# The second product of a fused FFN kernel turned round: weights stationary, activations moving, in 64x64 tiles

## The chip, the cores and the metric

The kernel runs on one core of a Trainium2 chip. The metric is the device time of one execution in microseconds. The kernel before takes 2056.47 us, the median of three runs (2056.41 to 2056.66).

## What is computed

Two layers in a row, all inputs and outputs in float32. The first is a short dynamic convolution: for each of 32768 tokens and each of 8 heads a softmax over 7 taps weighs the last 7 rows of x. The second is a feed-forward layer with a squared ReLU:

```python
w = softmax(weight_gen)                      # (8, 4096, 8, 7)
out = einsum('bshk,bskhg->bshg', w, x_unf)   # (8, 4096, 192): 7 taps, 24 channels to a head
h = out.reshape(32768, 192) @ w_in           # first product, (32768, 2048)
g = maximum(h, 0) ** 2
y = g @ w_out                                # second product, (32768, 192)
```

The accuracy of float32 is kept by splitting each factor into a high and a low float16 part. Each product is then the sum of three float16 products (high by high, low by high, high by low).

## The kernel before

**Tiling.** Token row `p * 256 + r` lies on partition `p`, so a partition holds 256 consecutive tokens. A chunk is `TC` = 4 values of `r`, or 512 tokens, and there are `NCH` = 64 chunks. Each chunk `c` has four blocks `b` = 0 to 3, and each block has two units `j`; a unit covers 256 of the 2048 hidden columns.

**The work of one unit.**
- `mm1(c, j)` (L412) makes the first product on TensorE. The 192 channels are folded to 64 partitions times 3, so each matmul has 64 rows, and the two halves `i` of the array (rows 0 to 63 and 64 to 127) make two blocks of hidden columns at once. The weights `W` are stationary (64x128), the transposed activations `xh`, `xl` move, 512 tokens wide.
- ScalarE does `relu` (L431), `square` (L435) and `high` (L439, the high float16 part `gh`). VectorE does `low` (L443, the low part `gl`).
- `mm2(c, b)` (L458) makes the second product for both units of a block. Here the activations `gh`, `gl` are stationary (64x128, 128 tokens wide) and the weights `V` move, 192 output channels wide. The result lies with tokens on the partitions. The two halves `h` of the hidden block go to the two row halves of the array and to two PSUM banks of the accumulator `acc[t // 2]`.

**The end of a chunk.** `finish(c, p)` (L482) runs once for each of the two accumulators. ScalarE copies one bank out, scaled by `f` (L493, into `tmp`); VectorE adds the other bank, scaled by `f`, and writes `o_sb` (L494). `f` is a scale for each partition, made by `descale` (L147). `store` (L496) issues one DMA for the chunk.

**The convolution of a later chunk** runs on VectorE in between: softmax steps (L289 to L293), seven multiplications and six additions of 128x768 (L306, L312), then from chunk 4 on a transpose in 32x32 blocks (L394), a round trip through DRAM to complete the transpose (`xd`, L400, and `xT`, L405), and the split into `xh` on ScalarE (L346) and `xl` on VectorE (L352). Chunks 0 to 3 are transposed on TensorE instead (L375), in float32, with weights of 128x64: two column halves of the array at once.

**The order of the work** is written out by hand in the last loop (L660 to L713). Every engine runs its instructions in that order. In iteration (c, b): the two `mm1` of the block; on VectorE the two `low` left over from the block before (`late`); if b = 1, the two `finish` and the `store` of chunk c - 1; then `mm2` of the block before; then the ScalarE steps; then the pieces of the convolution that a table (`todo`) has for this place. So `mm2(c, 0)` stands behind `finish(c - 1)` and needs its accumulators, which have one buffer each. All DMAs are issued on SyncE's queue (SP), in order.

Of the kernel before, what the change touches and what calls it, by code (L numbers as in the profile page):

```python
# [8 lines left out]
F32 = mybir.dt.float32  # L9
# [20 lines left out]
def kernel(  # L30
# [9 lines left out]
    nc = tc.nc  # L40
# [87 lines left out]
    def size_steps(gi):  # L128
# [15 lines left out]

        return total, scales

    def descale(gi):  # L147
        f = falls[gi] = att.tile([P, 1], F32, name="f", bufs=3)
        d = downs.pop(gi)
        stt(out=f, in0=d, scalar=back, in1=d, op0=ALU.mult, op1=ALU.mult)  # L150

    raws = {}

# [254 lines left out]


    phs, rgs, ghs, gls, accs = {}, {}, {}, {}, {}  # L410

    def mm1(c, j):  # L412
        ph = phs[c, j] = ps_h.tile([P, 2, N], F32, name="ph")
        if c == 0:
            w = wfull[j // 2].rearrange("p j n -> p (j n)").rearrange("p (k j n) -> p k j n", k=ND, j=2)
            seq = [(w, xts[0]["x"], k) for k in range(ND)]
        else:
            xh, xl = xts[c]["h"], xts[c]["l"]
            seq = [(W[:, q, j // 2], xx, k) for q, xx in ((0, xh), (0, xl), (1, xh)) for k in range(ND)]
        for n, (w, xx, k) in enumerate(seq):  # L420
            for i in range(2):
                rows = slice(i * D1, (i + 1) * D1)
                fl = dict(start=(n == 0), stop=(n == len(seq) - 1))
                nc.tensor.matmul(ph[:, i], w[rows, k, j % 2], xx[rows, k], **fl)  # L424

    def relu(c, j):
        r = rgs[c, j] = gp.tile([P, 2, N], F32, name="g", bufs=NJ)
# [27 lines left out]
            o = accs[0][t // 2][:, t % 2, 0:D]  # L455
            nc.tensor.matmul(o, rgs[0, j][:, i, t * P:(t + 1) * P], v, start=fb == 0, stop=fb == NF - 1)  # L456

    def mm2(c, b, ts_=range(TC)):  # L458
        if b == 0 and 0 in ts_:
            new_accs(c)  # L460
        j0, j1 = 2 * b, 2 * b + 1
        order = [(t, j) for t in ts_ for j in (j0, j1)]
        if c == NCH - 1 and b == NB - 1:
            order = [(t, j) for j in (j0, j1) for t in range(TC)]
        for t, j in order:
            for i in range(2):
                fb = block(j, i)
                first, last = fb == 0 and t % 2 == 0, fb == NF - 1 and t % 2 == 1
                for n, g in enumerate((ghs[c, j], ghs[c, j], gls[c, j])):
                    for h in range(2):  # L470
                        rows = slice(h * D1, (h + 1) * D1)
                        nc.tensor.matmul(  # L472
                            accs[c][t // 2][:, h, t % 2 * D:(t % 2 + 1) * D],
                            g[rows, i, t * P:(t + 1) * P], V[rows, fb, n * D:(n + 1) * D],
                            start=first and n == 0, stop=last and n == 2,
                        )
        for j in (j0, j1) if TC - 1 in ts_ else ():
            del ghs[c, j], gls[c, j]

    outs = {}  # L480

    def finish(c, p):  # L482
        if p == 0:
            outs[c] = op.tile([P, TC, D], F32, name="o_sb")
        o = outs[c][:, 2 * p:2 * p + 2]
        acc = accs[c][p]
# [5 lines left out]
        tmp = op.tile([P, 2 * D], F32, name="tmp")  # L492
        act(tmp, acc[:, 1, 0:2 * D], AF.Copy, scale=f)  # L493
        stt(out=o, in0=acc[:, 0, 0:2 * D], scalar=f, in1=tmp, op0=ALU.mult, op1=ALU.add)  # L494

    def store(c, p0=0, p1=2):  # L496
        nc.sync.dma_start(
# [162 lines left out]
    for c in range(1, NCH + 1):  # L660
        for b in range(NB if c < NCH else 2):
# [20 lines left out]
            if b == 1:  # L682
                for p in range(2):
                    finish(c - 1, p)
                    if c == NCH:
                        store(c - 1, p, p + 1)
                if c < NCH:
                    store(c - 1)
            turn = turns.pop(c + 1, None) if b == NB - 1 else None
            if b == NB - 1 and c + 1 in splits and turn is None:  # L690
# [3 lines left out]
                mm2(*pend.pop(0))  # L694
            elif pend:
                one = pend.pop(0)
                mm2(*one, range(TC // 2))
                turn()
                mm2(*one, range(TC // 2, TC))
            if c < NCH:  # L700
                relu(c, js[0])
                square(c, js[0])
# [41 lines left out]
```

## Time and profile before

The profiled execution took 2056.41 us, 2054.6 us of it from the first to the last instruction (the span).

| engine | busy us | share of the span |
|---|---|---|
| TensorE, matmul (PE) | 2044.6 | 100% |
| TensorE, weight load (PEld) | 1492.7 | 73% |
| VectorE (DVE) | 1762.3 | 86% |
| ScalarE (ACT) | 1755.1 | 85% |
| the 16 DMA engines, hardware queue | | 25.2% |

Busy times of matmuls overlap, since several run in the array at once and each is recorded to the end of its pipeline. How fast they follow each other is read from when groups start. Rows named PEld are weight loads. In a row such as `64*128 64x192 f16`, the first pair is the part of the array (rows by columns), the second is what moves through it (partitions by columns). SPq is SyncE's queue; its rows are the issue of DMAs, not the transfers.

### The profile page before, as it was taken

To read this page: it belongs to the slowest core of one execution; us is meant where nothing else is said; L and a number is where in the kernel's file an instruction comes from. 1 tells how busy PE (TensorE), PEld (TensorE's weight loads), DVE (VectorE), ACT (ScalarE), POOL (GpSimd) and SP (SyncE) were. 2 spreads that over 40 slices of the span, in tenths; PEclk is the share of its full clock that TensorE was granted. 3 is DMA by queue.
4 is the path that set the end of the run, shared out by engine and by line. 5 is a ranking of instruction groups with operands and counts; after the bars stand their busy time and mean duration, and the time that the engine had idled before them with its cause. 6 is when DMAs were issued, how large, how long until landed. Compare 5 with 4: busy or idle time off the path is not lost.

```text
span 2054.6 us, 73890 instructions
## 1 busy us (share of the span) xinstructions
PE 2044.6 (100%) x33814; PEld 1492.7 (73%) x33814; DVE 1762.3 (86%) x2310; ACT 1755.1 (85%) x2010; POOL 10.5 (1%) x14
## 2 busy tenths in 40 slices
PE   9999999999999999999999999999999999999999
PEld 6777777777777777777777777777777777777777
DVE  8999888888888888888888888888888888888873
ACT  6788888888888888888888888888888888888887
POOL 2000000000000000000000000000000000000000
PEclk9999999999999999999999999999999999999999
DMA  6112221332312322213323123222133231232220
GB/s 186 41 63 81 87 65 62 95 95 64 95 41 86 95 72 87 77 51 94 95 64 95 45 82 95 72 87 83 45 95 92 67 95 48 80 95 72 56 63 18
DMA packets 98073, 158.34 MB, mean 77 GB/s; under 512 B 8168, under 2 KB 60776, under 8 KB 93792
## 3 DMA queue, kind: packets, MB, share of 16 engines
q1 hardware_dynamic: 97760, 153.61, 25.2%
q8 instruction: 264, 4.33, 0.9%
q14 instruction: 49, 0.40, 0.1%
HBM read 104.82 MB, written 48.76 MB: 75 GB/s over the span
## 4 chain that ended last, share of the span: by engine, by line
PE 98%; DVE 2%; SPq 0%; DMA 0%; issue 0%; ACT 0%; POOL 0%; DVEq 0%; POOLq 0%
PE acc L472 49%; PE ph L424 48%; PE acc L456 1%; DVE pr L306 0%; DVE pr L312 0%; PE ph L375 0%; DVE W L262 0%; SPq L117 0%; DMA xt<-in_x_dram 0%; DVE gl L443 0%; DVE xl L352 0%; DVE du L199 0%; ACT xh L346 0%; DVE V L262 0%; DVE o_sb L494 0%
## 5 line engine op out<-in xcount | busy, mean ns | idle before, releaser
L472 PE MATMUL acc<-V,gh 64*128 64x192 f16 x16128 | 1018.5, 243 | 0.0
L472 PE MATMUL acc<-V,gl 64*128 64x192 f16 x8064 | 991.7, 243 | 0.2 <-DVE gl L443 0.2
L443 DVE SCALAR_TENSOR_TENSOR gl<-gh,g 128x1024 f16<-128x1024 f16 x504 | 613.2, 1223 | 232.8 <-ACT gh L439 232.6
L424 PEld LDWEIGHTS <-W 64*128 64x128 f16 x9072 | 437.6, 94 | 478.8 <-DVE xl L352 0.8
L424 PE MATMUL ph<-xh,W 64*128 64x512 f16 x6048 | 776.3, 376 | 0.5 <-DVE xl L352 0.5
L472 PEld LDWEIGHTS <-gh 64*128 64x128 f16 x16128 | 728.7, 94 | 59.8 <-issue 0.3
L431 ACT ACTIVATE g<-ph 128x1024 f32<-128x1024 f32 x504 | 511.0, 1014 | 252.7 <-PE ph L424 252.6
L435 ACT ACTIVATE g<-g 128x1024 f32<-128x1024 f32 x512 | 538.8, 1052 | 8.1
L439 ACT ACTIVATE gh<-g 128x1024 f16<-128x1024 f32 x504 | 530.1, 1052 | 8.0
L306 DVE TENSOR_TENSOR pr<-xt,wt 128x768 f32<-128x768 f32 x449 | 421.4, 951 | 2.9 <-DMA xt<-in_x_dram 0.8
L424 PE MATMUL ph<-xl,W 64*128 64x512 f16 x3024 | 408.7, 376 | 0.0
L472 PEld LDWEIGHTS <-gl 64*128 64x128 f16 x8064 | 392.5, 94 | 0.5 <-DVE gl L443 0.5
L312 DVE TENSOR_TENSOR pr<-pr 128x768 f32<-128x768 f32 x384 | 364.5, 949 | 2.3
L352 DVE TENSOR_TENSOR xl<-xT,xh 128x512 f16<-128x512 f32 x180 | 113.5, 685 | 21.0 <-ACT xh L346 21.0
L346 ACT CAST xh<-xT 128x512 f16<-128x512 f32 x180 | 98.4, 609 | 0.0
L494 DVE SCALAR_TENSOR_TENSOR o_sb<-acc,f,tmp 128x384 f32<-128x384 f32 x126 | 71.6, 609 | 3.3 <-ACT tmp L493 3.3
L493 ACT ACTIVATE tmp<-acc,f 128x384 f32<-128x384 f32 x126 | 65.2, 566 | 3.3 <-PE acc L472 3.3
L394 DVE STREAM_TRANSPOSE xr<-pr 128x768 f32<-128x768 f32 x60 | 58.7, 978 | 2.1
L137 ACT ACTIVATE junk<-xt 128x1536 bf16<-128x1536 f32 (+1 forms) x32 | 47.3, 1478 | 0.0
L286 DVE SCALAR_TENSOR_TENSOR wt<-wt,up,sm 128x224 f32<-128x224 f32 x63 | 28.5, 452 | 2.2
L291 ACT ACTIVATE wt<-wt 128x224 f32<-128x224 f32 x64 | 24.0, 375 | 7.3 <-DVE wt L290 7.2
L290 DVE TENSOR_TENSOR wt<-wt,mx 128x224 f32<-128x224 f32 x64 | 25.1, 392 | 2.2
(66 smaller groups left out, 326.0 us busy)
## 6 DMA issues: line engine op xcount, KB each, us to landing
xT<-xd SPq DMA_DIRECT2D x120, 384.0 KB, 5.0
xt<-in_x_dram SPq DMA_DIRECT2D x31, 1344.0 KB, 9.2
out_dram<-o_sb SPq DMA_DIRECT2D x63, 384.0 KB, 5.5
xd<-xr SPq DMA_DIRECT2D x240, 96.0 KB, 2.1
wt<-in_weight_gen_dram SPq DMA_DIRECT2D x31, 224.0 KB, 5.8
raw<-in_moe_w_in_dram SPq DMA_DIRECT2D x8, 384.0 KB, 9.6
raw<-in_moe_w_out_dram SPq DMA_DIRECT2D x4, 768.0 KB, 4.4
xt<-in_x_dram SPq DMA_DIRECT2D x2, 384.0 KB, 5.2
```

The costliest lines, as they stand in the source:

```text
L306: tt(out=dst, in0=src, in1=wk.broadcast_to([P, (t1 - t0) * H, G]), op=ALU.mult)
L312: tt(out=prs[k0][:, part], in0=prs[k0][:, part], in1=prs[k][:, part], op=ALU.add)
L346: nc.scalar.copy(xh, xs)
L352: tt(out=xl, in0=xs, in1=xh, op=ALU.subtract)
L424: nc.tensor.matmul(ph[:, i], w[rows, k, j % 2], xx[rows, k], **fl)
L431: act(r, phs.pop((c, j)), AF.Relu, scale=RHO * LIFT ** 0.5)
L435: act(r, r, AF.Square)
L439: act(gh, rgs[c, j], AF.Copy, scale=1.0 / LIFT)
L443: stt(out=gl, in0=ghs[c, j], scalar=-LIFT, in1=rgs.pop((c, j)), op0=ALU.mult, op1=ALU.add)
L472: nc.tensor.matmul(accs[c][t // 2][:, h, t % 2 * D:(t % 2 + 1) * D], g[rows, i, t * P:(t + 1) * P], V[rows, fb, n * D:(n + 1) * D], start= ...
L493: act(tmp, acc[:, 1, 0:2 * D], AF.Copy, scale=f)
L494: stt(out=o, in0=acc[:, 0, 0:2 * D], scalar=f, in1=tmp, op0=ALU.mult, op1=ALU.add)
```

## The change

It concerns chunks 4 to 62 (`turned`). In these, `mm2_turned` makes the second product with `V` as the stationary operand in pieces of 64x64, and `gh`, `gl` moving. The output channels now lie on the partitions. 128 of the 192 channels go through four matmuls with 512 tokens each (two row halves by two column halves of the array, into `accs[c][0]`); the last 64 channels go through four matmuls with 256 tokens each, one column half for each half of the tokens (into `accs[c][1]`). `mm1` of these chunks is cut into 64x64 pieces too, so all matmuls use one tiling.

`finish` no longer scales. ScalarE copies one bank to `tmp`, VectorE adds the other and writes `s`, 512 columns for the first accumulator and 256 for the second. `store_turned` then turns `s` in 32x32 blocks on VectorE, multiplies by the scale, and stores in 24 DMAs whose contiguous pieces are 32 floats. The scale is needed in another layout (`fs`), which `descale` makes by one DMA to DRAM and four back, for each group of two chunks. `mm2` can now be split by unit where it was split by token tile.

```diff
     def descale(gi):
...
+        if gi * CPG >= N_PE:
+            fd = dram.tile([P], F32, name="fd")
+            fs = spread_falls[gi] = att.tile([P, 1, P // Q, 1], F32, name="fs", bufs=3)
+            nc.sync.dma_start(out=fd.rearrange("(p a) -> p a", a=1), in_=f)
+            for m in range(P // Q):
+                nc.sync.dma_start(
+                    out=fs[m * Q:(m + 1) * Q, 0, :, 0], in_=fd.rearrange("(q i) -> i q", i=Q)
+                )
...
+    HALVES = slice(0, D1), slice(D1, P)
+    def turned(c):
+        return N_PE <= c < NCH - 1
     def mm1(c, j):
...
+        cols = HALVES if turned(c) else (slice(0, P),)
         for n, (w, xx, k) in enumerate(seq):
-            for i in range(2):
-                rows = slice(i * D1, (i + 1) * D1)
-                fl = dict(start=(n == 0), stop=(n == len(seq) - 1))
-                nc.tensor.matmul(ph[:, i], w[rows, k, j % 2], xx[rows, k], **fl)
+            fl = dict(start=(n == 0), stop=(n == len(seq) - 1))
+            for col in cols:
+                for i in range(2):
+                    rows = HALVES[i]
+                    nc.tensor.matmul(ph[col, i], w[rows, k, j % 2, col], xx[rows, k], **fl)
...
+    def mm2_turned(c, j):
+        if j == 0:
+            new_accs(c)
+        gh, gl = ghs.pop((c, j)), gls.pop((c, j))
+        for i in range(2):
+            fb = block(j, i)
+            for n, g in enumerate((gh, gh, gl)):
+                fl = dict(start=fb == 0 and n == 0, stop=fb == NF - 1 and n == 2)
+                for col in HALVES:
+                    for r, rows in enumerate(HALVES):
+                        d = n * D + col.start
+                        nc.tensor.matmul(accs[c][0][col, r], V[rows, fb, d:d + D1], g[rows, i], **fl)
+                for m, col in enumerate(HALVES):
+                    for r, rows in enumerate(HALVES):
+                        d = n * D + P
+                        nc.tensor.matmul(
+                            accs[c][1][col, r, 0:N // 2], V[rows, fb, d:d + D1],
+                            g[rows, i, m * N // 2:(m + 1) * N // 2], **fl,
+                        )
...
     def finish(c, p):
+        acc = accs[c][p]
+        if turned(c):
+            if p == 0:
+                sums_t[c] = op.tile([P, TC * D], F32, name="s", bufs=1)
+            n0, n1 = ((0, N), (N, N + N // 2))[p]
+            n = n1 - n0
+            tmp = op.tile([P, N], F32, name="tmp")
+            nc.scalar.copy(tmp[:, 0:n], acc[:, 1, 0:n])
+            tt(out=sums_t[c][:, n0:n1], in0=acc[:, 0, 0:n], in1=tmp[:, 0:n], op=ALU.add)
+            return
...
+    def store_turned(c):
+        o = op.tile([P, TC * D], F32, name="o_sb")
+        nc.vector.transpose(o, sums_t.pop(c))
+        ob = o.rearrange("p (a q j) -> p a q j", q=P // Q, j=Q)
+        tt(out=ob, in0=ob, in1=spread_falls[c // CPG].broadcast_to(ob.shape), op=ALU.mult)
+        for col in range(0, D, Q):
+            for t in range(TC):
+                if col < P:
+                    p0, n0 = col, t * P
+                else:
+                    p0, n0 = 2 * t // TC * D1 + col - P, N + t % 2 * P
+                nc.sync.dma_start(
+                    out=out_v[:, c * TC + t, col:col + Q].rearrange("(q i) j -> i q j", i=Q),
+                    in_=o[p0:p0 + Q, n0:n0 + P].rearrange("i (q j) -> i q j", j=Q),
+                )
```

Three places show how the instructions move. The first is TensorE where a first product ends and the second product of the block before begins, in the middle of the kernel. Before (L424 is `mm1`, L472 is `mm2`):

```order
L424 MATMUL ph<-xh,W 128x512
L472 LDWEIGHTS gh
L472 MATMUL acc_17189<-V,gh 128x192
L472 LDWEIGHTS gh
L472 MATMUL acc_17189<-V,gh 128x192
L472 LDWEIGHTS gh
L472 MATMUL acc_17189<-V,gh 128x192
L472 LDWEIGHTS gh
L472 MATMUL acc_17189<-V,gh 128x192
L472 LDWEIGHTS gl
L472 MATMUL acc_17189<-V,gl 128x192
```

and now (L440 is `mm1`, L485 and L489 are `mm2_turned`; the lines of the changed file are further down):

```order
L440 MATMUL ph<-xh,W 64x512
L485 LDWEIGHTS V
L485 MATMUL acc_18595<-gh,V 64x512
L485 LDWEIGHTS V
L485 MATMUL acc_18595<-gh,V 64x512
L485 LDWEIGHTS V
L485 MATMUL acc_18595<-gh,V 64x512
L485 LDWEIGHTS V
L485 MATMUL acc_18595<-gh,V 64x512
L489 LDWEIGHTS V
L489 MATMUL acc_18596<-gh,V 64x256
```

What was eight matmuls of 192 columns for one 128-column block of hidden units and one of the three terms is now four of 512 and four of 256; both accumulators are written from the start of the block.

The second place is VectorE at the end of a chunk, in block b = 1 of the next one. Before:

```order
L443 SCALAR_TENSOR_TENSOR gl<-gh,g 128x1024 x2
L494 SCALAR_TENSOR_TENSOR o_sb<-acc_20468,f,tmp 128x384
L494 SCALAR_TENSOR_TENSOR o_sb<-acc_20469,f,tmp 128x384
L292 TENSOR_REDUCE sm<-wt 128x32
L293 TENSOR_SCALAR sm<-sm 128x32
L293 RECIPROCAL sm<-sm 128x32
```

and now:

```order
L459 SCALAR_TENSOR_TENSOR gl<-gh,g 128x1024 x2
L532 TENSOR_TENSOR s<-acc_24412,tmp 128x512
L532 TENSOR_TENSOR s<-acc_24413,tmp 128x256
L548 STREAM_TRANSPOSE o_sb<-s 128x768
L550 TENSOR_TENSOR o_sb<-o_sb,fs 128x768
L302 TENSOR_REDUCE sm<-wt 128x32
L303 TENSOR_SCALAR sm<-sm 128x32
L303 RECIPROCAL sm<-sm 128x32
```

Two instructions became four, in the same place; what follows them is as before.

The third is SyncE's queue over two chunks. Before:

```order
L400 DMA xd<-xr 32x6x128 x4
L405 DMA xT<-xd 64x3x512 x2
L497 DMA out_dram<-o_sb 128x768
L109 DMA wt<-in_weight_gen_dram 128x448
L110 DMA xt<-in_x_dram 128x2688
```

and now:

```order
L415 DMA xT<-xd 64x3x512 x2
L557 DMA out_dram<-o_sb 32x4x32 x24
L156 DMA fd<-f 128x1
L158 DMA fs<-fd 32x4x1 x4
L410 DMA xd<-xr 32x6x128 x4
L415 DMA xT<-xd 64x3x512 x2
L557 DMA out_dram<-o_sb 32x4x32 x24
L109 DMA wt<-in_weight_gen_dram 128x448
L110 DMA xt<-in_x_dram 128x2688
```

One store became 24, and in every second chunk the five small transfers of the scale stand between a chunk's stores and the next chunk's `xd`.

More of the change, by code (lines that the diff above doesn't have):

```diff
@@ L145, in size_steps @@
         return total, scales
+    spread_falls = {}
     def descale(gi):
@@ L456, in mm2_first, with mm2 @@
             nc.tensor.matmul(o, rgs[0, j][:, i, t * P:(t + 1) * P], v, start=fb == 0, stop=fb == NF - 1)
-    def mm2(c, b, ts_=range(TC)):
+    def mm2_turned(c, j):
[17 more added lines that the diff above has]
+                        )
+    def mm2(c, b, half=None):
+        j0, j1 = 2 * b, 2 * b + 1
+        if turned(c):
+            for j in (j0, j1) if half is None else (j0 + half,):
+                mm2_turned(c, j)
+            return
+        ts_ = range(TC) if half is None else range(half * TC // 2, (half + 1) * TC // 2)
         if b == 0 and 0 in ts_:
             new_accs(c)
-        j0, j1 = 2 * b, 2 * b + 1
         order = [(t, j) for t in ts_ for j in (j0, j1)]
@@ L478, in mm2 @@
             del ghs[c, j], gls[c, j]
-    outs = {}
+    outs, sums_t = {}, {}
     def finish(c, p):
+        acc = accs[c][p]
+        if turned(c):
+            if p == 0:
[5 more added lines that the diff above has]
+            tt(out=sums_t[c][:, n0:n1], in0=acc[:, 0, 0:n], in1=tmp[:, 0:n], op=ALU.add)
+            return
         if p == 0:
@@ L485, in finish @@
         o = outs[c][:, 2 * p:2 * p + 2]
-        acc = accs[c][p]
         if c == 0:
@@ L491, in finish @@
         o = o.rearrange("p t d -> p (t d)")
-        tmp = op.tile([P, 2 * D], F32, name="tmp")
-        act(tmp, acc[:, 1, 0:2 * D], AF.Copy, scale=f)
-        stt(out=o, in0=acc[:, 0, 0:2 * D], scalar=f, in1=tmp, op0=ALU.mult, op1=ALU.add)
+        tmp = op.tile([P, N], F32, name="tmp")
+        act(tmp[:, 0:2 * D], acc[:, 1, 0:2 * D], AF.Copy, scale=f)
+        stt(out=o, in0=acc[:, 0, 0:2 * D], scalar=f, in1=tmp[:, 0:2 * D], op0=ALU.mult, op1=ALU.add)
+    def store_turned(c):
[13 more added lines that the diff above has]
+                )
     def store(c, p0=0, p1=2):
@@ L686 @@
                         store(c - 1, p, p + 1)
-                if c < NCH:
+                if turned(c - 1):
+                    store_turned(c - 1)
+                elif c < NCH:
                     store(c - 1)
@@ L696 @@
                 one = pend.pop(0)
-                mm2(*one, range(TC // 2))
+                mm2(*one, 0)
                 turn()
-                mm2(*one, range(TC // 2, TC))
+                mm2(*one, 1)
             if c < NCH:
```

## The prediction, made before the changed kernel was run

> **What bounds the kernel now.** I read the page's busy line first, then the chain that ended last, then that chain as a list in time, and only then single rows.
>
> ```profile
> PE 2044.6 (100%) x33814; PEld 1492.7 (73%) x33814; DVE 1762.3 (86%) x2310; ACT 1755.1 (85%) x2010; POOL 10.5 (1%) x14
> PE 98%; DVE 2%; SPq 0%; DMA 0%; issue 0%; ACT 0%; POOL 0%; DVEq 0%; POOLq 0%
> ```
>
> The chain is TensorE from end to end. As a list (start, length, what), from the middle of the kernel:
>
> ```profile
> 1007.14 3.96 PE acc L472 x96
> 1011.11 3.88 PE ph L424 x36
> 1014.99 3.96 PE acc L472 x96
> ...
> 1054.21 3.96 PE acc L472 x96
> ```
>
> A block is 36 matmuls of the first product (3.88 us) and 96 of the second (3.96 us), with nothing in between: 7.845 us, four to a chunk. Other engines matter only where they would make TensorE wait. Whether it streams at full rate is read from the steps. Two matmuls run side by side, one in each row half. So the first product makes 18 steps of 512 columns in 3.88 us, 215.6 ns each; the second makes 48 steps of 192 columns in 3.965 us (1007.14 to 1011.11 and 1014.99 to 1018.95), 82.6 ns each. Between them lie 320 columns and 133 ns: 0.416 ns a column, and 2.8 ns that every step costs whatever its width.
>
> **TensorE after the change.** The columns stay the same. For one block of hidden units and one term, before: 4 steps of 192 = 768 columns; after, if four 64x64 matmuls run side by side: one step of 512 and one of 256 = 768. Only the number of steps falls, from 48 to 24 in a block's second product. A step of 256 takes 256 x 0.416 + 2.8 = 109.2 ns, so the second product takes 12 x (215.6 + 109.2) = 3.90 us in place of 3.965: 0.067 us less. The first product has twice the matmuls, four in a step instead of two, and the same 18 steps: no change. 59 chunks (4 to 62) have 236 blocks: 236 x 0.067 = 15.8 us. That is all there is to gain.
>
> It needs two things that this kernel does not do now: four matmuls at once, and weight loads of 64 columns hidden beneath them. The nearest rows are TensorE's transposes of the early chunks, with two column halves at once, and the loads of today:
>
> ```profile
> 10.01 0.14 PEld L375 LDWEIGHTS acc<-ident,pr 128*64 128x64 f32 x2 [0.97 <-DVE pr L312]
> 10.01 0.33 PE L375 MATMUL acc<-ident,pr 128*64 128x128 f32 x2 [0.78 <-DVE pr L312]
> ...
> 58.29 2.84 PE L375 MATMUL ph<-ident,pr 128*64 128x128 f32 x48 [0.67 <-DVE pr L312]
> ...
> 1008.05 0.10 PEld L472 LDWEIGHTS <-gl 64*128 64x128 f16 x2
> ...
> L472 PEld LDWEIGHTS <-gh 64*128 64x128 f16 x16128 | 728.7, 94 | 59.8 <-issue 0.3
> L375 PEld LDWEIGHTS acc<-ident,pr 128*64 128x64 f32 x144 | 7.8, 137 | 2.0 <-DVE pr L312 1.9
> L375 PE MATMUL ph<-ident,pr 128*64 128x128 f32 x144 | 8.5, 274 | 0.7 <-DVE pr L312 0.7
> L456 PEld LDWEIGHTS acc<-du,g 128*128 128x128 f32 x128 | 20.7, 190 | 1.4 <-DVE du L198 0.8 <-issue 0.6
> ```
>
> Two loads into different column halves, each of 137 ns or so, lie within 0.14 us: they start some 7 ns apart and run together. Two loads into different row halves, 94 ns each, lie within 0.10 us. The 48 float32 matmuls last 2.84 us: with the length of the last one, 0.27 us, taken off, 24 pairs at 107 ns, which is 128 columns at twice 0.416 ns. So two column halves stream at full rate, with a load of 64 columns for each pair member in every 107 ns, though one load takes 137: loads run ahead. A step of 256 lasts 109 ns and asks for the same in each column half, with the two row halves beside it, as today. How many ns a load holds up the next one is therefore 2 to 7 by these rows; four of them, 28 ns, fit under 109. The other end: 64 columns more make a load 53 ns longer (137 to 190). If loads stood in line with 53 ns each, four would take 212 ns, which fits under a step of 512 and not under one of 256. I take the near end, full rate.
>
> [...]
>
> **VectorE and ScalarE.** The rows for the finish, first the durations and then VectorE's tightest place, just ahead of the 1054.21 above:
>
> ```profile
> L494 DVE SCALAR_TENSOR_TENSOR o_sb<-acc,f,tmp 128x384 f32<-128x384 f32 x126 | 71.6, 609 | 3.3 <-ACT tmp L493 3.3
> L352 DVE TENSOR_TENSOR xl<-ph,xh 128x512 f16<-128x512 f32 x9 | 5.7, 684 | 7.8 <-ACT xh L346 7.8
> L306 DVE TENSOR_TENSOR pr<-xt,wt 128x768 f32<-128x768 f32 x447 | 420.3, 953 | 2.9 <-DMA xt<-in_x_dram 0.8
> L306 DVE TENSOR_TENSOR pr<-xt,wt 128x384 f32<-128x384 f32 x2 | 1.1, 550 | 0.0
> L394 DVE STREAM_TRANSPOSE xr<-pr 128x768 f32<-128x768 f32 x60 | 58.7, 978 | 2.1
> L493 ACT ACTIVATE tmp<-acc,f 128x384 f32<-128x384 f32 x126 | 65.2, 566 | 3.3 <-PE acc L472 3.3
> L340 ACT COPY xT<-acc 128x512 f32<-128x512 f32 x3 | 1.7, 587 | 0.2 <-PE acc L375 0.2
> ```
>
> ```profile
> 1024.93 1.23 DVE L443 SCALAR_TENSOR_TENSOR gl<-gh,g 128x1024 f16<-128x1024 f16 x1 [1.16 <-ACT gh L439]
> 1026.97 1.23 DVE L443 SCALAR_TENSOR_TENSOR gl<-gh,g 128x1024 f16<-128x1024 f16 x1 [0.81 <-ACT gh L439]
> ...
> 1043.72 1.23 DVE L443 SCALAR_TENSOR_TENSOR gl<-gh,g 128x1024 f16<-128x1024 f16 x1 [0.41 <-ACT gh L439]
> ...
> 1052.44 1.13 DVE L494 SCALAR_TENSOR_TENSOR o_sb<-acc,f,tmp 128x384 f32<-128x384 f32 x2
> ...
> 1056.32 1.22 DVE L443 SCALAR_TENSOR_TENSOR gl<-gh,g 128x1024 f16<-128x1024 f16 x1 [0.37 <-ACT gh L439]
> 1058.35 1.22 DVE L443 SCALAR_TENSOR_TENSOR gl<-gh,g 128x1024 f16<-128x1024 f16 x1 [0.81 <-ACT gh L439]
> ...
> 1000.00:1031.40 31.40, 31.40 (x534) 22.87 (x530) 26.97 (x34) 26.55 (x31) 0.00 (x0) 1.00 0.21 54
> 1031.40:1062.80 31.40, 31.40 (x534) 22.87 (x530) 27.63 (x39) 27.90 (x33) 0.00 (x0) 1.00 0.28 78
> ```
>
> Removed: 2 x 609. Added: 684 for the addition of 512 columns out of PSUM; 684 - 256 x 1.05 = 415 for that of 256 (1.05 ns a column from 953 and 550); 978 for the turn; 953 for the scaling. Together 3.03 us for 1.22, 1.81 more in a chunk. The windows' third figure is VectorE's busy time: 26.97 and 27.63 of 31.4, so 28.8 and 29.4 of about 31.1. It still fits.
>
> Where it could bite is order. `finish` frees the accumulators for the next chunk's second product: it ends at 1053.57, TensorE starts at 1054.21, 0.64 us to spare. The two additions take 1.10 us where the two instructions took 1.22, so the release does not move; but both accumulators are now written from the first steps, where the second was not touched for 2 us. Turn and scaling stand behind the release. What they push back is the softmax and the `gl` of the block: 1.8 us meet waits of 0.37 and 0.81 in one kind of chunk and 1.16 and 0.81 in the other. The 0.6 us left over meets the margin of `gl`, which ends at 1059.6 and is wanted at 1062.1, and the waits of the next blocks. So the cost is nothing; without that cover it would be 1.8 us x 59 = 106 us. I put 1 us in the sum for waits here and there. ScalarE: 587 and at most 566 for 2 x 566, at the same place, no change.
>
> **SyncE and the DMAs.** Around the same stores, and a transfer in small pieces (`xd`, 768 pieces of 512 bytes) alone:
>
> ```profile
> 992.83 0.53 SPq L110 DMA_DIRECT2D xt<-in_x_dram  x1
> ...
> 1034.69 1.47 ACT L137 ACTIVATE junk<-xt 128x1536 bf16<-128x1536 f32 x1
> ...
> 1049.59 1.79 SPq L400 DMA_DIRECT2D xd<-xr  x4
> 1054.69 1.24 SPq L405 DMA_DIRECT2D xT<-xd  x2
> 1055.98 0.59 SPq L497 DMA_DIRECT2D out_dram<-o_sb  x1
> 1056.61 0.43 SPq L109 DMA_DIRECT2D wt<-in_weight_gen_dram  x1
> 1057.08 0.69 SPq L110 DMA_DIRECT2D xt<-in_x_dram  x1
> 1079.90 1.80 SPq L400 DMA_DIRECT2D xd<-xr  x4
> ...
> q1 hardware_dynamic: 832, 0.39, 45.6%
> xd<-xr SPq DMA_DIRECT2D x4, 96.0 KB, 2.1
> ```
>
> 24 stores for one, each again of 128 pieces: 24 x 0.59 = 14.2 us of issue. The queue has 24 us between 1055.98 and the next `xd` at 1079.90, which therefore stays on time; the five small transfers of the scale (five times 0.43, and twice a landing of 2.1) fit in the remaining 10, and the scale is read three chunks later. The loads `wt`, `xt` start 14 us later; the first two rows show one issued at 992.8 and first read at 1034.7, so they have the time. A store is now 3072 pieces of 128 bytes, 192 to each DMA engine. Those 832 packets took 45.6% of 16 engines for 3.5 us, about 31 ns each. A piece of 128 bytes should take no longer, but no row shows it. At 31 ns they are 6 us, beside 0.21 to 0.28 of 31.4 us, some 7.7 us, that the engines work now. They fill 31.1 us only at 122 ns a piece, four times the row. Nothing on the path.
>
> **Sum.** 2054.6 (span) - 15.8 + 1 = 2039.8; with the 1.8 us around the span (2056.41 less 2054.6; the profiled run is at the median of 2056.47) about 2042 us.
>
> **The rivals.**
> - B: VectorE's backlog reaches the accumulators. For it: 0.64 us of margin, 1.7 us idle left in a chunk. Against: the idle stretches lie between finish and finish. It decides once the extra is above about 3 us. If TensorE then waits 0.4 us in each chunk: 59 x 0.4 = 24, 2066 us.
> - C: four weight loads do not run together. A step of 256 takes 212 ns, the second product 12 x (215.6 + 212) = 5.13 us, 1.17 more in a block, x 236 = 275: about 2332 us. It decides above 27 ns for each load in line (109 / 4). Against: the 7 ns above.
> - D: pieces of 128 bytes cost more than 122 ns; the DMA engines become the bound, and `xT` comes late. At 150 ns: 7.7 + 28.8 = 36.5 us a chunk, +5.4 x 59: about 2360 us.
> - E: four in a step cost more than two. The 2.8 ns did not grow from one row half to two column halves, but if each matmul paid its own, a step would cost 8.4 more, a block 42 x 8.4 = 0.35: +83 - 16, 2123 us. At 1.6 ns more the gain is gone, 2056 us.
>
> **How the numbers follow.** Forecast 0.62 (2036 to 2050), B 0.12, C 0.13, D 0.06, E 0.07. A measurement of this kernel tells 0.2%, 4 us, from no change. Faster: 0.62, a quarter of B and two in seven of E, 0.67. Same: 0.07, from B and E. Slower: C, D and the rest of B and E, 0.26. The range 2035 to 2100 leaves out C, D and the far end of E, 0.20.
>
> **What would show it.** In the list of the chain: second products of 3.90 us and first ones of 3.88, four matmuls of 512 starting within some 10 ns. C: 256-wide steps of about 200 ns. B: waits of TensorE for VectorE's additions. D: waits for `xT`, a DMA share near 1. E: first products above 3.88. The forecast is wrong if either product's time grows.

## The result, and the profile after

The changed kernel took 2077.3 us (median, 2076.66 to 2084.55), the kernel before 2056.44 us beside it: a ratio of 1.0109 (95% interval 1.0087 to 1.0132). Slower by 1.1%, where faster was forecast. Run again in two later jobs, unchanged, it took 2056.6 us (1.0000, 0.9991 to 1.0010) and 2057.74 us (1.0005, 0.9995 to 1.0014): neither faster nor slower. With nothing altered but that the 128 words of the scale lie 16 bytes apart in DRAM, it takes 2042.94 us (0.9935, 0.9920 to 0.9949). So the gain that was forecast is there, and a small transfer that was costed at nothing eats it, and in the first job more than it.

The profiled execution of the first job took 2084.55 us, 2082.8 of them its span. It is the longest of that job's four (the other three took 2076.66 to 2077.68 us, with a mean granted clock of 0.998 where this one had 0.995). Its page, the busy line and the shares of the chain that ended last:

```profile
PE 2047.9 (98%) x42310; PEld 1744.4 (84%) x42310; DVE 1864.4 (90%) x2428; ACT 1750.4 (84%) x2010; POOL 10.2 (0%) x14
PE 95%; DVE 3%; issue 1%; SPq 0%; DMA 0%; ACT 0%; POOL 0%; DVEq 0%; POOLq 0%
```

TensorE was the chain at 98% and is now at 95%. "Issue" is time in which an engine waits for nothing that the profile shows. The waits, longest in total first (total us, times, longest), have it on the lines of TensorE's second product (L485 and L489, in steps of 512 and 256), where the kernel before had 0.3 us; L440 is the first product:

```profile
PEld L485 <- issue: 17.7, 13, 2.9
PE acc L485 <- issue: 15.8, 11, 2.6
PEld L489 <- issue: 10.2, 7, 2.6
```

The chain as a list in time (start, length, what) shows one such place, and an undisturbed first product behind it:

```profile
998.42 1.89 issue
1000.31 0.41 PE acc L489 x4
1000.72 0.43 PE acc L485 x4
...
1007.86 0.22 PE acc L485 x4
1008.07 0.11 PE acc L489 x4
1008.18 0.22 PE acc L485 x4
...
1011.43 3.89 PE ph L440 x72
```

Undisturbed, a first product lasts 3.89 us, a step of 512 lasts 0.22 us and one of 256 lasts 0.11 us. Here TensorE stands still for 1.89 us, and then its steps last twice as long. The windows say why: the columns are length, then busy time of PE, PEld, DVE, ACT and POOL with instructions, then TensorE's granted clock, DMA share and GB/s.

```profile
998.40:1000.30 1.90, 0.02 (x1) 0.01 (x1) 1.87 (x4) 1.87 (x3) 0.00 (x0) 1.00 0.00 0
1000.30:1005.00 4.70, 4.69 (x68) 3.91 (x71) 3.17 (x5) 0.94 (x3) 0.00 (x0) 0.64 0.06 4
1005.00:1012.00 7.00, 7.00 (x160) 6.19 (x156) 5.51 (x9) 5.95 (x6) 0.00 (x0) 1.00 0.69 164
```

TensorE is empty while VectorE and ScalarE work on, the DMA engines carry next to nothing, and behind the gap the granted clock is 0.64 in the mean: one stretch of 3.41 us at 0.5. What lies just ahead of the gap is on SyncE's queue:

```profile
991.89 0.34 SPq L156 DMA_DIRECT2D fd<-f  x1
1000.36 1.74 SPq L158 DMA_DIRECT2D fs<-fd  x4
1002.19 1.86 SPq L410 DMA_DIRECT2D xd<-xr  x4
```

`fd` is 128 words of 4 bytes, one from each partition, written side by side in DRAM. The next instruction of the queue, which reads them back, goes out 8.5 us later, and over all 30 trips 7.7 to 9.1, 8.3 in the median. The view of line 156 has the landing itself for three of the 30 trips:

```profile
DMA to landing us min/median/max: 8.3/8.7/8.7
```

In the packet records the words themselves are under way early: all 4-byte packets of this trip start 0.84 to 1.04 us after the issue, 9 ns each. The view takes a DMA as landed with the last of 16 updates of its semaphore. In the three trips for which the trace has all 16, the first comes 3.0 to 3.3 us after the issue and the others follow one after another, up to the 8.3 to 8.7 of the view. In that time the 16 KB packets of the instruction queue get long: 26 of 330 take over 1.9 us, up to 4.1, where the kernel before has none over 1.86 us, and 24 of the 26 start between the issue of an `fd` and its landing. The chain shows 24.4 us of gaps behind the trips, 21 of them, behind 16 of the 30; those over half a microsecond begin 6.0 to 7.6 us after `fd` is issued. The seven over 1.5 us end 8.4 to 8.8 us after it, within 0.7 us of the moment its reads go out. In six places a stretch at half clock follows (0.5 for 3.41 us), each costing an estimated half of its 3.41 us, 10 us together; behind gaps of 1.88 and 2.27 us none follows.

Added up by blocks: undisturbed, a block starts 7.785 us after the one before. What the blocks take beyond that is 42.3 us in all. Some 0.9 us of it are there in every form, without the trip too (e1); the rest lies in blocks shortly after an `fd`. Gaps and clock make up 34.6 us, and the other 7 or so the chain books on TensorE's own lines.

### The profile page after: what moved, and what is told of

It is laid out like the page before. It is cut to its first block, busy times and chain, and to the rows that moved or that the text cites. A ratio compares the mean times of both kernels' runs of the same rounds, so it can differ in the third digit from the quotient of the medians.

```text
span 2082.8 us, 92659 instructions
## 1 busy us (share of the span) xinstructions
PE 2047.9 (98%) x42310; PEld 1744.4 (84%) x42310; DVE 1864.4 (90%) x2428; ACT 1750.4 (84%) x2010; POOL 10.2 (0%) x14
## 3 DMA queue, kind: packets, MB, share of 16 engines
q1 hardware_dynamic: 314768, 153.79, 30.2%
## 4 chain that ended last, share of the span: by engine, by line
PE 95%; DVE 3%; issue 1%; SPq 0%; DMA 0%; ACT 0%; POOL 0%; DVEq 0%; POOLq 0%
PE ph L440 48%; PE acc L485 34%; PE acc L489 9%; PE acc L513 3%; DVE pr L316 1%; DVE pr L322 0%; DVE du L208 0%; DVE du L209 0%; DVE du L207 0%; PE ph L385 0%; DVE W L272 0%; SPq L117 0%; DMA xt<-in_x_dram 0%; DVE gl L459 0%; DVE xl L362 0%
## 5 line engine op out<-in xcount | busy, mean ns | idle before, releaser
L440 PEld LDWEIGHTS <-W 64*64 64x64 f16 (+1 forms) x17568 | 762.5, 107 | 208.7 <-issue 4.5
L440 PE MATMUL ph<-xh,W 64*64 64x512 f16 (+1 forms) x11712 | 882.7, 377 | 0.8 <-DVE xl L362 0.5
L485 PE MATMUL acc<-gh,V 64*64 64x512 f16 x7552 | 805.6, 377 | 13.4 <-issue 13.4
L485 PEld LDWEIGHTS <-V 64*64 64x64 f16 x11328 | 645.9, 107 | 76.1 <-issue 17.7
L489 PE MATMUL acc<-gh,V 64*64 64x256 f16 x7552 | 696.7, 270 | 4.1 <-issue 4.0
L489 PEld LDWEIGHTS <-V 64*64 64x64 f16 x11328 | 645.2, 107 | 22.7 <-issue 10.2
L485 PE MATMUL acc<-gl,V 64*64 64x512 f16 x3776 | 497.8, 378 | 2.5 <-issue 2.5
L440 PE MATMUL ph<-xl,W 64*64 64x512 f16 (+1 forms) x5856 | 477.7, 377 | 0.0
L489 PE MATMUL acc<-gl,V 64*64 64x256 f16 x3776 | 395.7, 270 | 1.3 <-issue 1.3
L513 PE MATMUL acc<-V,gl 64*128 64x192 f16 x512 | 63.5, 243 | 2.9 <-issue 2.6
L513 PE MATMUL acc<-V,gh 64*128 64x192 f16 x1024 | 65.3, 243 | 0.0
```

Source lines behind the costliest of these rows:

```text
L440: nc.tensor.matmul(ph[col, i], w[rows, k, j % 2, col], xx[rows, k], **fl)
L485: nc.tensor.matmul(accs[c][0][col, r], V[rows, fb, d:d + D1], g[rows, i], **fl)
L489: nc.tensor.matmul(accs[c][1][col, r, 0:N // 2], V[rows, fb, d:d + D1], g[rows, i, m * N // 2:(m + 1) * N // 2], **fl,)
L513: nc.tensor.matmul(accs[c][t // 2][:, h, t % 2 * D:(t % 2 + 1) * D], g[rows, i, t * P:(t + 1) * P], V[rows, fb, n * D:(n + 1) * D], start= ...
```

## The experiments

**Is it the trip through DRAM?** First without it, then with the words far apart.

```diff
# e1_no_trip
-            nc.sync.dma_start(out=fd.rearrange("(p a) -> p a", a=1), in_=f)
-            for m in range(P // Q):
-                nc.sync.dma_start(out=fs[...], in_=fd.rearrange("(q i) -> i q", i=Q))
+            nc.gpsimd.memset(fs[:, 0, :, 0], 1.0)
# e2_512B_apart; e3_64B_apart, e5_16B_apart and e10_8B_apart have 16, 4 and 2 for 128
-            fd = dram.tile([P], F32, name="fd")
+            fd = dram.tile([P, 128], F32, name="fd")
-            nc.sync.dma_start(out=fd.rearrange("(p a) -> p a", a=1), in_=f)
+            nc.sync.dma_start(out=fd[:, 0:1], in_=f)
-                    in_=fd.rearrange("(q i) -> i q", i=Q)
+                    in_=fd[:, 0].rearrange("(q i) -> i q", i=Q)
```

> The changed kernel without the five small DMAs of the scale (fd, fs): fs is filled with ones, so the outputs of chunks 4 to 62 lack their scale. Theory T (the whole loss is TensorE running out of instructions while the 4-byte words of fd are being written to DRAM): no gap of TensorE put down to issue, clock 1.000, blocks of 7.785 us throughout; span about 2082.8 - 41.6 = 2041 us, time about 2043. Rival R (the fetch is late because there are more instructions and 24 stores a chunk, and fd only falls in the same place): gaps stay, time 2070 to 2085.

Measured: 2043.22 us (0.9934, 0.9917 to 0.9950), and no gaps. All of the loss is in these five DMAs.

> The changed kernel with the words of fd 512 bytes apart in DRAM instead of side by side; output unchanged. If it is that 128 words of 4 bytes go to the same few lines of DRAM and are written one after the other (T1): fd lands in about 2 us instead of 8.7, no gaps, about 2043 us. If any write of 4-byte words is slow (T2): landing stays near 8.7 us, time stays 2076 to 2085. Rival R: gaps stay whatever fd does.

Measured: 2043.14 us (0.9934, 0.9919 to 0.9949). The same five DMAs with the same number of 4-byte packets, and the loss is gone: 0.9 us beyond the pace of 7.785 in a block. `fd` now lands after 2.3 us in the median; in every one of the 30 trips 15 of the 16 updates are in by 1.5 us.

> As the run with 512 bytes, with the words 64 bytes apart. T1 with a line of 64 bytes or less: landing about 2 us, 2043 us, as with 512 bytes. T1 with a longer unit (256 or 512 bytes): landing in between, 3 to 6 us, and some gaps left. T2: as the changed kernel, 2076 to 2085.

Measured: 2043.17 us (0.9935, 0.9920 to 0.9949), landing again 2.3 us. Its view of line 156, and then its chain in the list of time:

```profile
DMA to landing us min/median/max: 1.4/2.3/3.6
```

```profile
1028.39 3.88 PE ph L440 x72
1036.18 3.88 PE ph L440 x72
1043.96 3.88 PE ph L440 x72
```

A block every 7.785 us with nothing lost. No instruction packet takes over 1.78 us.

> The changed kernel with the words of fd 16 bytes apart, four to a stretch of 64 bytes; output unchanged. fd landed in 8.7 us side by side (16 words to 64 bytes) and in 2.3 us at 64 bytes apart, 6.4 us more for 128 words. P (the stretches of 64 bytes work side by side, the words of one wait for each other): 4/16 of the 6.4, landing about 3.9 us, hardly a gap, 2043 to 2048 us. Q (every word after the first of a stretch waits, all in one line): 96 words x 50 ns = 4.8, landing about 7.1 us, gaps, 2055 to 2075 us.

Measured: 2042.94 us (0.9935, 0.9920 to 0.9949), landing 2.3 us. Both expectations for this spacing were too high.

> The words of fd 8 bytes apart, the whole a stretch of 1024 bytes; output unchanged. At 16 bytes apart (2048 bytes) nothing was left of the slow landing, side by side (512 bytes) it was 8.7 us. U (a stretch of some 512 bytes of DRAM takes its words one after the other, and the others work beside it): two stretches of 64 words, landing about 4 to 5 us, few gaps, 2043 to 2050 us. V (only words that are direct neighbours wait for each other): landing 2.3 us, 2043 us.

Measured: 2042.90 us (0.9934, 0.9919 to 0.9949), landing 3.0 us, between the two expected values, and 6 instruction packets over 1.9 us. Eight words to a stretch of 64 bytes leave the time where 64 bytes between the words put it (0.9934 and 0.9935); with 4 bytes, where no gap is left between the words, the landing was 8.7 us in the first job, in place of 3.0.

**Is it DRAM, or 4-byte neighbours as such?** The form with 64 bytes between the words, and one more DMA that writes the same 128 words side by side into SBUF.

```diff
+            row = att.tile([1, P], F32, name="row", bufs=2)
+            nc.sync.dma_start(out=row.rearrange("o (p a) -> o p a", a=1), in_=f)
```

> The kernel with the words of fd 64 bytes apart, and ahead of them one more DMA of the same 128 words, side by side, into one partition of SBUF, not used. X (it is DRAM that takes such words slowly): that DMA lands in 2 us or so, no gaps, 2043 us. Y (a DMA of 128 neighbouring words is slow wherever it writes, for instance in the DMA engines): landing 7 to 9 us, gaps, 2070 to 2085 us.

Measured: 2042.86 us (0.9934, 0.9917 to 0.9951); that DMA lands after 2.5 us and leaves no gap. The same words side by side took 8.7 us to land in DRAM in the first job, and 2.5 us in SBUF here.

**Does the kernel before mind the same trip?** It gets the five DMAs, whose result it does not use; then the same with its first product cut into 64x64 matmuls, which gives TensorE the changed kernel's number of instructions.

```diff
# e4_before_trip, in descale of the kernel before; e7_before_halves_trip the same on e6
+        if gi * CPG >= N_PE:
+            fd = dram.tile([P], F32, name="fd")
+            fs = att.tile([P, 1, P // Q, 1], F32, name="fs", bufs=3)
+            nc.sync.dma_start(out=fd.rearrange("(p a) -> p a", a=1), in_=f)
+            for m in range(P // Q):
+                nc.sync.dma_start(out=fs[...], in_=fd.rearrange("(q i) -> i q", i=Q))
# e6_before_halves, in mm1 of the kernel before
+            for col in cols:
+                for i in range(2):
+                    rows = halves[i]
+                    nc.tensor.matmul(ph[col, i], w[rows, k, j % 2, col], xx[rows, k], **fl)
```

> The kernel before, with the five small DMAs of the scale added and their result unused. T: fd lands in 8 to 9 us here too; TensorE uses its instructions more slowly here (528 loads and matmuls of each kind in 31.4 us against 672 in 31.1), so its store of them lasts longer: 0 to 10 us lost, 2056 to 2066. R: fd has nothing to do with it, no gap, 2056.

Measured: 2057.42 us (1.0004, 0.9994 to 1.0013). Landing 7.3 us (the reads go out after 7.1), and 26 of 264 instruction packets over 1.9 us, as in the changed kernel; but the chain has no gaps, and the waits on the second product's line (L480 here) are as good as none:

```profile
DMA to landing us min/median/max: 6.8/7.3/7.7
PEld L480 <- issue: 0.8, 4, 0.3
```

A slow landing alone costs this kernel 0.9 us by the medians, which is within the interval.

> The kernel before with one part of the change alone: the first product of chunks 4 to 62 in pieces of 64x64, the second as before in 64x128. Each block then changes the tiling twice. M (a change of tiling waits for the array to run empty, some 160 ns, the tail of a 512-wide matmul): 236 x 2 x 0.16 = 76 us, about 2132 us. N (no cost): the first product's steps stay at 215.6 ns, 2056 to 2057 us.

Measured: 2110.67 us (1.0264, 1.0249 to 1.0280). The price of a switch is lower than expected. The second product is still in 64x128 pieces, so TensorE switches tiling twice in a block, and the chain has both products longer, 4.01 and 4.07 us for 3.88 and 3.96. The chain, and then the waits, which name the place, 0.4 us at most each time:

```profile
1003.95 4.01 PE ph L427 x72
1007.96 4.07 PE acc L475 x96
```

```profile
PEld L475 <- issue: 97.4, 238, 0.4
PEld L427 <- issue: 37.4, 237, 0.2
```

A block takes 0.23 us more than 7.845, so a switch takes about 0.115 us. These waits say "issue" too, and are something else: they come with every block.

> The same with the five small DMAs of the scale as in the change (words of fd side by side), their result unused. TensorE now uses 1344 instructions a chunk, as in the changed kernel, with the second product, VectorE's work and the stores of the kernel before. T (the gaps come from the rate at which instructions are used and the time that fd blocks their fetch): gaps of TensorE put down to issue 6 to 9 us after fd, 20 to 40 us above the run without the trip. If the gaps need the 24 stores or the weights of the new second product: no gap, the time of the run without the trip.

Measured: 2125.35 us (1.0333, 1.0316 to 1.0350), 14.7 us more than e6, below the range expected. Landing 7.3 us as in e4 (the reads go out after 7.2), but now TensorE stands still 15 times after a trip, 13.1 us together by the chain, 5.9 to 7.2 us after `fd` is issued. The landing, and a row of the waits that e6 does not have:

```profile
DMA to landing us min/median/max: 7.2/7.3/7.4
PE acc L483 <- issue: 12.9, 13, 1.6
```

Between e4 and e7 only the cut of the first product differs: TensorE has more instructions, and it switches tiling, which costs e6 its 54 us without any such standstill. That points to the supply of instructions. The number of the 16 KB packets goes with TensorE's instructions: its 84620 loads and matmuls over 330 packets in the changed kernel, and 67628 over 264 in e4, are 256 to a packet in both, and e7, with 84620 as well and 6445 instructions of the other engines in place of 8039, has 330 too.

```profile
q8 instruction: 330, 5.41, 1.3%
```

```profile
q8 instruction: 264, 4.33, 1.0%
```

TensorE runs a load and a matmul for each of 672 pairs in 31.14 us after the change, 43.2 instructions a microsecond; a packet lasts 5.9 us. In e4 (528 pairs in 31.4 us) it lasts 7.6 us, in e7 (672 in 32.3) 6.2 us. If TensorE has about one packet ahead, a landing of 7.3 us is covered by 7.6 and not by 6.2, and in the first job no gap begins sooner than 6.0 us after `fd`. This is an estimate from these figures, not seen: no row says that TensorE lacked an instruction, or how many it has ahead.

The records even leave a doubt. At the place shown the last packet of instructions had ended at 996.75, 1.7 us before TensorE stopped, and in the standstill itself the DMA engines carry nothing (share 0.00). TensorE starts again about when `fd` has landed (1000.31, its reads go out at 1000.36), not when a recorded packet ends. What it waits for until then stays open.

**Is VectorE's cover as thin as predicted?** The form with 64 bytes between the words, with turn and scaling done a second time into another buffer.

```diff
+        o2 = op.tile([P, TC * D], F32, name="o2", bufs=1)
+        nc.vector.transpose(o2, sums_t.pop(c))
+        tt(out=ob2, in0=ob2, in1=spread_falls[c // CPG].broadcast_to(ob2.shape), op=ALU.mult)
```

> The changed kernel with the words of fd 64 bytes apart, and VectorE's turn and scaling made a second time into a tile that is not used (1.93 us more in a chunk). VectorE is busy 27.9 and 29.9 us in two chunks of 31.14 there, 28.9 in the mean; 30.9 with this. If VectorE's idle time can take all but some of it: TensorE waits a little in every second chunk, 2045 to 2060 us. If the order of the work leaves less cover than the busy time says (TensorE waiting for the accumulators in every chunk): above 2070. If the cover is wider: 2043.

Measured: 2042.97 us (0.9934, 0.9920 to 0.9949). Nothing, though the windows (VectorE is the third busy figure) have it filled to 30.7 and 30.2 of 31.14 us, and TensorE still at 31.14:

```profile
1000.00:1031.14 31.14, 31.14 (x678) 19.32 (x673) 30.70 (x40) 26.58 (x32) 0.00 (x0) 1.00 0.39 105
1031.14:1062.28 31.14, 31.14 (x678) 19.31 (x673) 30.24 (x43) 27.54 (x32) 0.00 (x0) 1.00 0.27 54
```

**Twice the words.** The changed kernel, with the words written side by side into two buffers.

```diff
+            fd2 = dram.tile([P], F32, name="fd2")
+            nc.sync.dma_start(out=fd2.rearrange("(p a) -> p a", a=1), in_=f)
```

> The changed kernel with the suspected cost doubled: the words are written to DRAM side by side twice, into two buffers, one DMA right behind the other. If the fetch of instructions is held up for as long as such words are being written, and the two stretches are served one after the other: landing about 16 us, TensorE out of instructions for some 8 us more at each of 30 places, 2300 us or more. If the two are served side by side: landing about 9 us and 2077 to 2085 us, as the changed kernel. If the words have nothing to do with it: the same, 2077 to 2085, at a landing of 16 us.

Measured: 2066.60 us (1.0046, 1.0031 to 1.0061). The one landing that the view has is 6.9 us; the reads go out 7.9 us after the first write and 7.5 after the second in the median. The two are served side by side, and sooner than the one of the first job, whose reads went out after 8.3. That does not fit a landing fixed by the layout.

**Does the landing go with the place or with the run?**

```diff
# e13_again: no edit
# e14_upper_half
-            fd = dram.tile([P], F32, name="fd")
+            fd = dram.tile([2 * P], F32, name="fd")
-            nc.sync.dma_start(out=fd.rearrange("(p a) -> p a", a=1), in_=f)
+            nc.sync.dma_start(out=fd[P:].rearrange("(p a) -> p a", a=1), in_=f)
```

> The changed kernel once more, unchanged. Its fd, 128 words side by side, landed 8.3 to 8.7 us after issue in the first run; with the words written to two buffers both landed after 6.9 us, and the time was 2066.6 instead of 2077.3 us. Theory place: the landing depends on where the buffer lies in DRAM, which goes with the program. Then it is 8.3 to 8.7 us again, with about 21 gaps put down to issue of 24 us together, and 2077 us (2074 to 2085). Theory run: it depends on the chip or the job. Then it lands after some 7 us here, with gaps of about 12 to 16 us together, and takes 2060 to 2068 us, like e14_upper_half beside it.

Measured: 2056.60 us (1.0000, 0.9991 to 1.0010). The same program, and the landing is 7.4 us, not 8.7 (the reads go out after 7.4, not 8.3). The view of line 156 and the waits:

```profile
DMA to landing us min/median/max: 7.4/7.4/7.7
```

```profile
PEld L485 <- issue: 7.6, 12, 1.6
PEld L489 <- issue: 4.7, 6, 1.4
PE acc L485 <- issue: 3.1, 9, 1.0
```

The gaps are shorter, none over 1.6 us, and the clock stays at 1.0 throughout: 13.9 us beyond the pace instead of 42.3. The landing goes with the run.

> The changed kernel with fd in the upper half of a buffer of 256 words, still side by side: only its place in DRAM is another. Theory place: a landing that differs from that of e13_again in the same job by over 1 us (6.9 against 8.5), and a time that goes with it, 2066 beside 2077. Theory run: the same landing as e13_again within 0.5 us and the same time within 5 us. On either theory gaps of TensorE appear wherever fd lands more than about 6.5 us after its issue, each about as long as the landing lasts beyond that.

Measured: 2055.49 us (0.9996, 0.9987 to 1.0005), 1.1 us from e13 in the same job; the reads of `fd` go out 7.36 us after it in the median, as in e13 (7.40). A place 512 bytes further on makes no difference.

> The changed kernel a third time, unchanged. It took 2077.3 us with a landing of fd of 8.7 us in the first job, and 2056.6 us with 7.4 us in e13_again. If the landing goes with the job or the chip, time and landing come out together once more: some 2055 us with 7.4, some 2077 with 8.7, and in between at about 16 us for each us of landing (20.7 us by 1.3 us). If the first job was a single stray, 2054 to 2059 us and 7.4 us again.

Measured: 2057.74 us (1.0005, 0.9995 to 1.0014), landing 7.4 us (the reads after 7.4), on another chip than e13. Two jobs agree; the first stands alone with 8.7 us, and time and landing went together all three times.

**What makes neighbours slow?** Two groups of 64 words a kilobyte apart; groups of 4 every 64 bytes; groups of 16 every 512 bytes.

```diff
# e16_two_halves
+            fd = dram.tile([2, 2 * P], F32, name="fd")
+            for n, rows in enumerate((slice(0, D1), slice(D1, P))):
+                nc.sync.dma_start(out=fd[n, 0:D1].rearrange("(p a) -> p a", a=1), in_=f[rows])
# e17_groups_of_4
+            fd = dram.tile([Q, 16], F32, name="fd")
+            nc.sync.dma_start(out=fd[:, 0:P // Q].rearrange("i q -> q i"), in_=f)
# e18_groups_of_16
+            fd = dram.tile([P // 16, P], F32, name="fd")
+            nc.sync.dma_start(out=fd[:, 0:16], in_=f)
```

> The 128 words of fd in two groups of 64, each group side by side, a kilobyte between the groups. Theory turns (the words of one stretch of DRAM are written one after the other, 7.4 to 8.7 us for 128, and two stretches run beside each other, as in e12_twice): the landing is 2.3 + half of the 5 to 6.4 us above that, 4.8 to 5.5 us, under the 6 us after which TensorE first stands still; no gaps or only short ones, 2043 to 2046 us. Rival, a fixed price for words side by side, however many: landing 7 us or more, and the time of e15_third_time beside it.

Measured: 2048.49 us (0.9959, 0.9945 to 0.9973), landing 6.8 us; the reads go out 6.6 us after the first of the two writes. Half as many words side by side land hardly sooner (7.4 us in e15 beside it), so the turns of one stretch do not add up as expected. But it is no price paid at once either: in the three landings on record the 16 updates come one after another, the first after 1.5 to 1.8 us.

> The 128 words of fd in groups of 4 side by side, a group every 64 bytes, so that a stretch of 64 bytes takes 4 words, as with words 16 bytes apart. Theory stretch (what counts is how many single words fall into one stretch of 64 bytes or more: 16 of 16 land after 7.4 us, 8 after 3.0, 4 or 1 after 2.3): landing 2.3 us, 2043 us. Rival neighbours (a word that directly follows another waits for it, however few they are, or the stretch is 16 bytes): landing 6 to 7.5 us and 2050 to 2058 us. Between them, a stretch of 32 bytes: 3.0 us and 2043 us.

Measured: 2043.00 us (0.9935, 0.9918 to 0.9951), no gaps. SyncE's queue sends the reads 2.5 us after `fd`:

```profile
1036.20 0.57 SPq L156 DMA_DIRECT2D fd<-f  x1
1038.69 1.72 SPq L158 DMA_DIRECT2D fs<-fd  x4
```

In the median of all trips it is 2.0 us. Groups of four neighbours cost this kernel nothing.

> Groups of 16 words side by side (64 bytes), a group every 512 bytes. Theory stretch of 64 bytes: 16 of 16 words as in the changed kernel, landing about 7 us and 2048 to 2058 us, though 512 bytes hold only 16 words. If the stretch is larger, 128 bytes and more, a stretch takes no more words than with 8 or 16 bytes between them: landing 2.3 to 3.0 us, 2043 us. Neighbours: 6 to 7.5 us as well.

Measured: 2043.07 us (0.9935, 0.9920 to 0.9950), no gaps, 2.4 us in the median from `fd` to its reads. Sixteen words filling 64 bytes cost nothing either; 64 words filling 256 bytes landed after 6.8 us and took 2048.49 us (e16). If it is a stretch of DRAM that takes its words slowly, it is larger than 64 bytes.

**Is the cut of the first product needed?** It adds instructions, of which TensorE seems to run short. The words 64 bytes apart, and the first product left in 64x128 pieces.

```diff
-        cols = HALVES if turned(c) else (slice(0, P),)
+        cols = (slice(0, P),)
```

> The words of fd 64 bytes apart (2043.2 us in that form), and the first product left as before, 64x128 pieces and half as many matmuls; only the second product is in 64x64 pieces, so the tiling switches twice in a block. Theory switch (0.115 us for each switch, from e6_before_halves): 236 blocks x 2 x 0.115 = 54 us more, about 2097 us, first and second products each some 0.11 us longer than 3.885 and 3.900. Rival, switching costs nothing and it is the half-width first product that costs: 2043 us.

Measured: 2096.84 us (1.0196, 1.0179 to 1.0213), as the price of a switch says. The chain has a first product of 3.99 us and the block at 8.02, and the waits come with every block again, 0.4 us at most:

```profile
1005.48 3.99 PE ph L440 x36
...
1013.50 3.99 PE ph L440 x36
```

```profile
PEld L485 <- issue: 100.1, 236, 0.4
PEld L440 <- issue: 72.1, 237, 0.3
```

Against 2043.17 us for e3, one tiling throughout is worth its instructions here.

## Why the prediction was wrong

**TensorE: right.** A block takes 3.885 + 3.900 us as worked out; against 7.845 that is 14.2 us over 236 blocks, and without the bad transfer the kernel gains 13.4 (2056.56 to 2043.17), with 2042 forecast. Four matmuls to a step kept the rate of two, 0.22 us for a step of 512 and 0.11 for one of 256: rivals C and E are out. The loads of 64 columns take 107 ns each, longer than the 94 of before, and lie under the steps (first row; the others belong to the next paragraph):

```profile
L485 PEld LDWEIGHTS <-V 64*64 64x64 f16 x11328 | 645.9, 107 | 76.1 <-issue 17.7
L532 DVE TENSOR_TENSOR s<-acc,tmp 128x512 f32<-128x512 f32 x59 | 40.4, 685 | 10.4 <-ACT tmp L531 10.4
L532 DVE TENSOR_TENSOR s<-acc,tmp 128x256 f32<-128x256 f32 x59 | 24.5, 416 | 0.0
L548 DVE STREAM_TRANSPOSE o_sb<-s 128x768 f32<-128x768 f32 x59 | 57.7, 978 | 2.0
L550 DVE TENSOR_TENSOR o_sb<-o_sb,fs 128x768 f32<-128x768 f32 x59 | 56.5, 958 | 2.0
```

The single load got longer, 107 ns for 64 columns where 128 took 94; but with four of them to each step a step of 256 still lasts 0.11 us, so they do not stand in line, and the step is not slowed.

**VectorE and ScalarE: right in the durations, too careful on the cover.** VectorE's four instructions took 685, 416, 978 and 958 ns, where 684, 415, 978 and 953 were forecast; ScalarE's two copies took 574 and 376, where 587 and at most 566 were. Rival B was to decide once the extra passed 3 us; e8 shows nothing at 1.81 + 1.93 us.

**The stores: right.** The 128-byte packets take 12.8 ns each in the mean, under half of the 31 allowed, and the hardware queue's share went from 25.2 to 30.2%. Rival D is out.

**The five small transfers: this step failed.** "The five small transfers of the scale (five times 0.43, and twice a landing of 2.1) fit in the remaining 10." The landing of 2.1 was taken from `xd`, pieces of 512 bytes, and `fd` is 128 words of 4 bytes: it landed after 8.7 us (7.4 in the later jobs). No rival had it. The way through SyncE's queue, which the prediction did look at, is not where it hurt: the next `xd` goes out 10.8 us after `fd` in the median, straight behind the reads, where in e3 it goes out after 7.4, but TensorE never waits for `xT`. What it left out was the other transfers of that time. The prediction asked who stands behind these DMAs on SyncE's queue and who reads their result, and not which packets of other queues are under way while `fd` is. The packets of the instruction queue took up to 4.1 us, where the kernel before has none over 1.86, and the seven standstills over 1.5 us ended 8.4 to 8.8 us after `fd`, about when it lands. That the slow write costs the time is shown (e1, e2, e3); that it does so by way of the instructions is inferred.

**And the change made TensorE sensitive to it.** The prediction counted the 168 matmuls of a block only as steps. In e4 the same landing costs 0.9 us; with 672 pairs of instructions in a chunk in place of 528 it costs 14.7 us (e7). In the changed kernel it costs 13.9 us, the whole gain, with a landing of 7.4 us, and 42.3 with 8.7 in the profiled execution (34 by the median of that job), an estimated 10 of these from the clock, which was 0.5 for 3.41 us behind six of the gaps.

The chance of 0.26 for slower was made of C, D, B and E, none of which occurred. That 2077.3 us lies within the range of 2035 to 2100 is luck: the range was drawn that wide for B and the near end of E.

**Open.** Why the landing was 8.7 us in the first job and 7.4 us in the two later ones (three landings on record in each; the reads behind them say 8.3 and 7.4 over all 30); which stretch of DRAM counts, if one does (an estimate from e10, e16 and e18: over 64 bytes, at most 256); and the supply of instructions is inferred from the lengthened packets and from e4 against e7, while the standstills end with the landing of `fd` and not with a recorded packet. Of the 26 long packets 10 start 7.2 us or more after `fd`, and end when its reads are already under way; no run separates the write side by side from reads side by side, though the standstills mostly begin before the reads go out. The stock of a packet orders the runs but does not size them: e12, whose reads go out 7.5 us after the second of two writes, lost 25.3 us, and e13, with 7.4 us after its one, 13.9.

## What to carry to other kernels

Take a small transfer's price from a row of the same shape, and where there is none, write the words with gaps: 16 bytes apart they cost this kernel nothing, side by side 13 to 34 us. When a step is called hidden, name every transfer that is under way in the same time (here, it seems, the packets of the instruction queue got longer), above all where the change raises the bounding engine's instructions per microsecond. And run a surprising result once more in another job before explaining its size: the sign itself hung on that here.

## What was unexpected of the hardware

The landing of 128 single words in DRAM, against their layout. Landing is the median from issue, with the number of trips for which the view has it; the reads wait for it, and the next column is the median time until they go out (in e16 after the first write). Long packets are instruction packets over 1.9 us. Loss is the time of all blocks beyond 7.785 us each; 0.9 us of it are there in every form, also without the trip.

| layout | landing us (trips) | reads go out us | long packets | loss us |
|---|---|---|---|---|
| side by side, first job (its longest execution) | 8.7 (3) | 8.3 | 26 | 42.3 |
| side by side, e13 and e15 | 7.4 (3 each) | 7.4, 7.4 | 28, 28 | 13.9, 13.7 |
| two groups of 64 side by side, e16 | 6.8 (3) | 6.6 | 25 | 7.6 |
| groups of 16, e18 | none | 2.4 | 0 | 0.9 |
| groups of 4, e17 | none | 2.0 | 1 | 0.9 |
| 8 bytes apart, e10 | 3.0 (30) | 3.0 | 6 | 0.9 |
| 64 bytes apart, e3 | 2.3 (30) | 2.3 | 0 | 0.9 |

In every layout the packets of the words have, in the median, all started 0.8 to 1.6 us after the issue; it is the end that comes late (side by side the 16 updates come one after another, up to 8.7 us; in e2 15 of them are in by 1.5 us), and with it come instruction packets of 1.9 to 4.1 us, where the median is 1.2 us. Beside it: a switch between 64x128 and 64x64 pieces cost TensorE an estimated 0.115 us (e6: 0.23 us more in a block of two switches; e9: a block of 8.02 us for 7.785); and in the first job's profiled execution the granted clock was 0.5 for 3.41 us behind six of the standstills, which turned a loss of 1.9 us at the place shown into an estimated 3.6, but not behind those of 1.88 and 2.27 us.
